# A reordered attention-and-mixer kernel: state by a casting load, dummy and half-width matmuls on TensorE, and state-token rows stored in (token, batch) order

## The chip, the cores and the metric

One core of a Trainium2 chip. The metric is device microseconds of one launch, median over runs. A launch is some 1.8 us longer than the span of its trace.

Some words of the profiles: PSUM is the memory that TensorE writes its results to, and the other engines copy (evacuate) them from there. The granted clock is TensorE's clock as a share of its full speed; in the rows of slices each digit is tenths (9 is 90% or more). The chain is the work that ended last, followed back step by step to what released it. The shape of a matmul's tile (128*128, 128*64 ...) is the part of TensorE's array that it uses.

## The reference

Eight batches, eight heads, 512 tokens and 32 state tokens of 64 features. Tokens attend to state and state attends to tokens (a softmax each); the two results are concatenated to 544 rows of 512 features, which go through a mixer:

```python
scores  = scale * x @ state.T ;  xread = softmax(scores)  @ state      # 512 rows
scores2 = scale * state @ x.T ;  sread = softmax(scores2) @ x          # 32 rows
y = concat([xread, sread], rows)                # (8, 544, 512) after merging heads
W_tok = scale * (y @ w_q) @ (y @ w_k).T         # 544 x 544 for each batch
out = relu(W_tok @ y) @ w_out                   # float32, (8, 544, 512)
```

## The kernel before

The schedule is written by hand: a list of tokens `step.batch.engine`, from which each engine gets its instructions in that order. TensorE (PE) is busy with matmuls, most of them small, for 79.8 of the 93.4 us; VectorE (DVE, `v`), ScalarE (ACT, `a`) and GpSimd (POOL, `p`) evacuate PSUM and do softmax work.

```python
ORDER = """
zst.0.p stc0.0.v stc1.0.a stt0.0.t xc0.0.p stt1.0.t xc1.0.a ste0.0.v ix1.0.p stf0.0.a xT0.0.t
stf1.0.v ix2.0.p ste1.0.a iwo.0.p xc2.0.v stb.0.t xc3.0.v ix3.0.p xTe0.0.v stbe.0.a xT1.0.t wc.0.p
...                                                             # cut
oe0.5.a fin1.6.t fin0.7.1 oe0.6.v oc0.7.a
"""
nc.sync.dma_start(out=st_f, in_=state...)         # whole state, 512 KB, (batch, head) on 64 partitions
...
def load(n, b, e):                                # ix: x of batch b, float32 to bf16 on the way
    nc.gpsimd.dma_start(out=x_bf[b], in_=xsrc(b, 0, H))
def st_tr(n, b, e):                               # 32 transposes of 64x64 for each half of the state
    ...
def st_back(n, b, e):                             # 16 transposes back, for the other layout
    ...
def fin_acc(ps, lhs):                             # one output piece: 128 rows, 512 columns
    for k in range(KC):
        nc.tensor.matmul(out=ps, lhsT=lhs(k), rhs=w_o[:, k, :], start=(k == 0), stop=(k == KC - 1))
def fs_ev(n, b, e):                               # state-token rows of four batches
    ...
    nc.sync.dma_start(out=out[4 * j : 4 * j + 4, S:SP, :], in_=ost)
```

`zst` clears a tile, `stt` and `ste/stf` transpose and evacuate the state, `xT` and `xTe` the same for x, `pt` makes scores, `exp` exponentiates, `srd` and `sums` read x by state, `wq`, `wks`, `wk`, `g`, `v`, `mix`, `mixs` are the mixer, `fin` and `fs` the output projections, `oe`, `oc`, `fse` their copies and stores.

The softmax here doesn't subtract the row's maximum and nothing guards it: scores larger than these inputs give would overflow.

## Time and profile before

| | before |
|---|---|
| time, median | 96.32 us (95.04 to 96.79); 96.0 to 96.1 us in the later sessions |
| span of the trace | 93.4 us |
| PE busy, granted clock over the span | 79.8 us (85%), 0.93 |
| batch 1's first transposes begin | 15.44 us |
| PE ends | 87.77 us |
| from there to the end | 5.6 us |

I read the last three rows as three stretches, start, middle and tail: 15.44 + 72.33 + 5.63 = 93.4.

### The profile page before, as it was taken

How to read it: one execution, taken by the hardware profiler on the slowest of the kernel's cores; microseconds unless marked ns; L12 is line 12 of the kernel's file. 1: busy time of each engine (PE TensorE's matmuls, PEld its weight loads, DVE VectorE, ACT ScalarE, POOL GpSimd, SP SyncE). 2: the span in 40 equal slices, each digit the busy share in tenths (PEclk: the TensorE clock that was granted, in tenths of full speed). 3: DMA queues.
4: the chain of work that ended last, by engine and by line, in shares of the span. 5: the costliest groups of instructions: out<-in, count | busy, mean ns of one | idle time of the engine just before them, and what ended most of it. 6: DMA issues, size and time to landing. Idle time of an engine off the chain costs nothing.

```text
span 93.4 us, 3134 instructions
## 1 busy us (share of the span) xinstructions
PE 79.8 (85%) x1376; PEld 53.4 (57%) x1376; DVE 56.2 (60%) x109; ACT 53.6 (57%) x80; POOL 44.6 (48%) x58
## 2 busy tenths in 40 slices
PE   5908098998995999999999999999999999999500
PEld 3506086896864676888366547646668644444100
DVE  1026948589584959896496198965786487222500
ACT  2324746687894687359967647864054876444200
POOL 7307994894499989899500009339750000000000
PEclk9998555599999999999999999999999999999985
DMA  1998799999999915500032517806455004428990
GB/s 28 305 260 193 94 160 156 205 203 194 197 199 197 201 18 232 225 11 0 0 130 102 225 22 213 311 30 270 186 225 232 0 0 164 173 39 300 400 363 21
DMA packets 12933, 15.13 MB, mean 162 GB/s; under 512 B 1592, under 2 KB 10296, under 8 KB 12856
## 3 DMA queue, kind: packets, MB, share of 16 engines
q0 software_dynamic: 7808, 4.19, 33.2%
q1 hardware_dynamic: 4280, 9.70, 29.3%
q10 hardware_dynamic: 832, 1.05, 3.8%
q8 instruction: 10, 0.16, 0.7%
q14 instruction: 3, 0.02, 0.1%
HBM read 10.22 MB, written 8.91 MB: 205 GB/s over the span
## 4 chain that ended last, share of the span: by engine, by line
PE 76%; ACT 6%; DMA 6%; DVE 4%; issue 2%; DVEq 0%
PE fin_ps L538 30%; PE xT_ps L246 9%; DMA st_f<-in_state_dram 6%; PE pt_ps L264 5%; PE mix_ps L504 5%; PE at_ps L322 4%; PE srd_ps L335 3%; PE wq_ps L398 3%; PE wk_ps L436 3%; DVE stT L139 3%; ACT xT L137 2%; PE fins_ps L538 2%; PE srd_ps L348 2%; PE v_ps L468 2%; PE g_ps L452 2%
## 5 line engine op out<-in xcount | busy, mean ns | idle before, releaser
L538 PE MATMUL fin_ps<-w_o,rmix 128*128 128x512 bf16 x128 | 30.0, 379 | 0.0
L309 POOL TENSOR_TENSOR A<-E,rinv 128x1024 bf16<-128x1024 bf16 (+1 forms) x9 | 15.3, 1718 | 15.5 <-DVE rinv L303 15.5
L538 PEld LDWEIGHTS <-rmix 128*128 128x128 bf16 x128 | 11.6, 98 | 12.5 <-ACT rmix L143 0.3
L137 ACT COPY ost<-fin_ps 128x1024 f32<-128x1024 f32 (+1 forms) x10 | 9.3, 928 | 14.1 <-PE fin_ps L538 13.6
L139 DVE COPY ost<-fin_ps 128x1024 f32<-128x1024 f32 (+1 forms) x8 | 8.7, 1089 | 11.1 <-PE fin_ps L538 7.5
L280 ACT ACTIVATE E<-pt_ps 128x512 bf16<-128x512 f32 x16 | 9.6, 603 | 4.3 <-PE pt_ps L264 4.3
L372 POOL TENSOR_TENSOR sbd<-srn,mask 128x256 bf16<-128x256 bf16 x16 | 9.5, 612 | 4.4 <-DVE srn L362 4.1
L295 DVE TENSOR_REDUCE rsum<-E 128x16 f32<-128x512 bf16 x16 | 10.6, 672 | 1.1 <-ACT E L280 1.1
L246 PE MATMUL xT_ps<-ident,x_bf 128*128 128x128 bf16 x128 | 11.0, 238 | 0.1
L145 DVE TENSOR_SCALAR rmix<-mix_ps 128x1024 bf16<-128x1024 f32 x7 | 8.5, 1223 | 2.7 <-PE mix_ps L504 2.6
L137 ACT COPY xT<-xT_ps 128x1024 bf16<-128x1024 bf16 x9 | 9.1, 1020 | 1.5 <-PE xT_ps L246 1.5
L143 ACT ACTIVATE rmix<-mix_ps 128x1024 bf16<-128x1024 f32 x9 | 9.3, 1032 | 0.7 <-PE mix_ps L504 0.5
L213 POOL TENSOR_TENSOR stbd<-st_bf,mask 128x256 bf16<-128x256 bf16 x16 | 9.3, 614 | 0.0
L246 PEld LDWEIGHTS <-x_bf 128*128 128x128 bf16 x128 | 8.4, 106 | 1.0 <-issue 0.4
L264 PE MATMUL pt_ps<-stT,xT 128*128 128x64 bf16 x128 | 7.1, 203 | 0.5 <-DVE xT L139 0.4
L504 PE MATMUL mix_ps<-wq,V 64*128 64x256 bf16 x64 | 5.7, 272 | 1.2 <-issue 1.1
L152 POOL DMA_DIRECT2D x_bf<-in_x_dram x7 | 6.6, 944 | 0.0
L264 PEld LDWEIGHTS <-xT 128*128 128x128 bf16 x128 | 5.6, 105 | 1.6 <-DVE xT L139 0.5
L139 DVE COPY xT<-xT_ps 128x1024 bf16<-128x1024 bf16 x7 | 4.8, 686 | 2.2 <-PE xT_ps L246 2.0
L139 DVE COPY AT<-at_ps 128x1024 bf16<-128x1024 bf16 x7 | 4.8, 685 | 1.2 <-PE at_ps L322 1.2
L322 PE MATMUL at_ps<-ident,A 128*128 128x128 bf16 x64 | 5.0, 219 | 0.0
L504 PEld LDWEIGHTS <-V 64*128 64x128 bf16 x64 | 2.4, 94 | 3.8 <-issue 2.8
(76 smaller groups left out, 115.9 us busy)
## 6 DMA issues: line engine op xcount, KB each, us to landing
out_dram<-ost SPq DMA_DIRECT2D x14, 512.0 KB, 3.8
x_bf<-in_x_dram POOLq DMA_DIRECT2D x7, 512.0 KB, 13.4
out_dram<-ost SPq DMA_DIRECT2D x4, 256.0 KB, 2.1
st_f<-in_state_dram SPq DMA_DIRECT2D x1, 512.0 KB, 5.6
x_f<-in_x_dram ACTq DMA_DIRECT2D x2, 256.0 KB, 4.3
x_f<-in_x_dram SPq DMA_DIRECT2D x2, 256.0 KB, 6.3
w_o<-in_moe_w_out_dram POOLq DMA_DIRECT2D x1, 512.0 KB, 10.5
out_dram<-ost ACTq DMA_DIRECT2D x2, 256.0 KB, 3.9
```

What stands on the lines that cost most here:

```text
L137: nc.scalar.copy(out=out, in_=in_)
L139: nc.vector.tensor_copy(out=out, in_=in_)
L143: nc.scalar.activation(out=out, in_=in_, func=AF.Relu)
L213: nc.gpsimd.tensor_tensor(out=stbd[:, b, r], in0=st_bf[:, b, r : r + 1, :].to_broadcast((128, NP, D)), in1=mask[:, :, None].to_broadcast(( ...
L246: nc.tensor.transpose(out=ps[:, u, q, :], in_=x_bf[b][:, NP * r + q, 128 * u : 128 * u + 128], identity=ident,)
L264: nc.tensor.matmul(out=ps[:, 2 * u : 2 * u + 2, NS * q : NS * q + NS], lhsT=L[b][f"xTe{r}"][:, u, q, :], rhs=stT[:, b, :, NP * r + q, :], ...
L280: nc.scalar.activation(out=L[b]["E"][:, r].rearrange("p c q n -> p c (q n)"), in_=L[b][f"pt{r}"], func=AF.Exp, scale=float(scale),)
L295: nc.vector.reduce_sum(out=L[b]["rsum"][:, w], in_=L[b]["E"].rearrange("p r c q n -> p (r c q) n")[:, w], axis=AX.X,)
L309: eng.tensor_tensor(out=L[b]["A"].rearrange("p r c q n -> p (r c q) n")[:, w], in0=L[b]["E"].rearrange("p r c q n -> p (r c q) n")[:, w], ...
L372: nc.gpsimd.tensor_tensor(out=L[b]["sbd"][:, r], in0=L[b]["srn"][:, r : r + 1, :].to_broadcast((128, NP, D)), in1=mask[:, :, None].to_broa ...
L504: nc.tensor.matmul(out=ps[:, h, kk, :], lhsT=L[b]["V"][rows, 128 * k : 128 * k + 128], rhs=L[b]["wq"][rows, 0:SH], start=True, stop=True,)
L538: nc.tensor.matmul(out=ps, lhsT=lhs(k), rhs=w_o[:, k, :], start=(k == 0), stop=(k == KC - 1))
```

## The change

The intent: shorten the start by a smaller first load of state and a shorter way of its transposes; keep PE's clock up by dummy matmuls; take fewer changes of PE's tile shape by splitting matmuls that stand beside half-width ones; spread the end; and let all DMA engines carry the state-token rows. Nearly every place in the order changes as well.

Cuts are marked by `...`; calls are shortened.

```diff
-    nc.sync.dma_start(out=st_f, in_=state...)             # 512 KB
+    st_src = state.rearrange("b (r q) n d -> (q n) (b r) d", r=2)
+    st_load(0, 1)                                         # batch 0, 64 KB; x of batch 0 follows
...
+    st_load(1, 3)                                         # 128 KB
+        elif n == "is":
+            nc.gpsimd.dma_start(out=st_bf[:, 3:B], in_=st_src[:, 6 : 2 * B])   # casting
...
-    for w in range(16):                                   # warm-up, 256 columns each
+    for w in range(8):                                    # 512 columns each
+    def fill(n, b, e):                                    # b dummy matmuls of 512 columns
+        ps = psA.tile([128, 512], FP, name="fill_ps", tag="psA")
+        for w in range(b):
+            nc.tensor.matmul(out=ps, lhsT=zero[:, 0:128], rhs=zero, start=True, stop=True)
...
+    def mm(m, out, lhsT, rhs, **kw):
+        if m == "c":                                      # two 64-column halves side by side
+            for h in range(2):
+                lh = lhsT[:, 2*h : 2*h+2, :] if len(lhsT.shape) == 3 else lhsT[:, 64*h : 64*h+64]
+                nc.tensor.matmul(out=out[64*h : 64*h+64], lhsT=lh, rhs=rhs, **kw)
...
-        nc.sync.dma_start(out=out[4*j : 4*j+4, S:SP, :], in_=ost)
+        nc.sync.dma_start(out=out[4*j : 4*j+4, S:SP, :].rearrange("b n e -> n b e"), in_=ost)
-    rmix_s = const.tile([128, 2, KC, 4, NS], BF, name="rmix_s")
+    rmix_s = const.tile([128, 2, KC, NS, 4], BF, name="rmix_s")
-    tail = ctx.enter_context(tc.tile_pool(name="tail", bufs=6))
+    tail = ctx.enter_context(tc.tile_pool(name="tail", bufs=7))
...
-zst.0.p stc0.0.v stc1.0.a stt0.0.t xc0.0.p ...            # the whole ORDER
+zst.0.p ix1.0.p stc.0.v xc1.0.a fill.1.t stt.0.c ste.0.v stbd.0.p stf.0.a xc0.0.p xc3.0.v ix2.0.p
+fill.7.t xT0.0.t xc2.0.v xTe0.0.a fill.1.t xT1.0.t is.0.p ...
+... fs.7.t mxe1.7.a fse.7.v fix1.7.t fix2.7.t oc1.7.a fix0.7.t oc2.7.a fix3.7.t oc0.7.a oc3.7.b
```

Both state-token stores now stand at the very end (`fse.3`, `fse.7`); one stood in the middle before. The last piece (`oc3.7.b`) is copied in two halves by DVE and ACT.

## The prediction

> **What bounds the kernel now.** I read the page's slices first, then the chain that ended last, then stretches of time, then the PE timeline, last the DMA view.
>
> The page's 40 slices (2.335 us each):
>
> ```profile
> PE   5908098998995999999999999999999999999500
> PEclk9998555599999999999999999999999999999985
> DMA  1998799999999915500032517806455004428990
> ```
>
> PE is busy in nearly every slice from the sixth on; it is the bound of the middle. But in slices 4 to 7 its clock is at half, and the first four and last three slices hold little useful PE work. The chain in order of time (start, length, what):
>
> ```profile
> 0.73 5.58 DMA st_f<-in_state_dram
> ...
> 7.08 0.71 PE stT_ps L180 x32
> ...
> 7.89 1.22 DVE stT L139
> 9.14 1.24 DVE stT L139
> 10.40 1.01 ACT stT L137
> 11.46 1.03 PE stb_ps L201 x16
> 12.49 0.98 PE xT_ps L246 x8
> ...
> 15.44 1.03 PE xT_ps L246 x8
> ...
> 79.94 7.81 PE fin_ps L538 x36
> 87.77 0.59 ACT ost L137
> ```
>
> So the start is a chain of latencies through the state: one 512 KB load, transposes, four evacuations, transposes back. The transposes of batch 1 begin at 15.44, where they also wait 0.3 us for their load. PE ends at 87.77, and 5.6 us of copy and store follow to 93.4. Three stretches, with busy time of PE, PEld, DVE, ACT and POOL, granted clock, DMA share and GB/s:
>
> ```profile
> 7.00:12.50 5.50, 3.02 (x89) 2.56 (x90) 4.23 (x6) 2.92 (x4) 4.85 (x7) 0.65 0.89 150
> 12.50:18.70 6.20, 5.81 (x133) 4.80 (x134) 3.62 (x8) 4.28 (x6) 4.68 (x7) 0.50 1.27 172
> 18.70:30.00 11.30, 9.72 (x290) 7.90 (x288) 8.05 (x19) 9.07 (x15) 8.69 (x13) 0.99 1.44 198
> ```
>
> From 12.5 to 18.7 PE is 94% busy at clock 0.50. From 18.7 to 30 the clock is full but PE is idle 1.6 us, with DVE, ACT and POOL at 70 to 80%. The start and the tail are what can still be won. The tail in the DMA view of 76 to 93.4 us (slices of 0.435 us), with the landing of the batch loads over the whole run:
>
> ```profile
> GB/s 0 0 0 0 0 202 386 396 221 0 33 381 188 38 19 14 24 71 99 160 207 395 396 424 443 377 414 424 405 179 424 419 386 381 254 71 5 0 0 0
> x_bf<-in_x_dram POOLq DMA_DIRECT2D x7, 512.0 KB, 13.4
> ```
>
> From about 85 to 91.5 us the stores run at some 400 GB/s: the last nine output pieces are made back to back and the queue is full when PE ends. Before that, from 81.6 to 83.8, only 14 to 160 GB/s move: that is the store of state-token rows issued at 80.58.
>
> **What the Trainium skill says.** "TensorE: Matmul & The Clock Gate", Part 1: the PE clock is 1.2 GHz by default and 2.4 GHz after about 3.4 us of sustained work. The trace agrees in the ratio: eight transposes take 0.45 us later, 1.03 us at 12.49. Part 4 of that page: transposes do not count as PE-busy in the same way. The trace fits: 12.5 to 18.7 is dense, largely transposes, and stays at 0.50. "TensorEngine Tiling (Array Packing)", Key Properties: changing tiling mode drains the array. The trace agrees, below, at about 0.10 us. "DMA: Bandwidth & Descriptors", on why a DMA increments its semaphore by 16: the slowest dimension of the access pattern limits how many of 16 engines carry it. The state-token store has 4 (batches) outermost, and its slow stretch fits four engines.
>
> **The change part by part.** PE timeline, start and duration; I take start to start as the cost:
>
> ```profile
> 36.37 0.41 PE L436 MATMUL wk_ps<-sw,AT 128*128 128x64 bf16 x8
> 36.71 0.42 PE L335 MATMUL srd_ps<-x_bf,E 128*32 128x64 bf16 x32
> 37.06 0.41 PE L398 MATMUL wq_ps<-AT,sw 128*64 128x256 bf16 x4
> 37.30 0.28 PE L407 MATMUL wq_ps<-srT,w_qk 128*64 128x32 bf16 x8
> ```
>
> The wk group takes 0.34 us before the srd group of another tile shape, 0.23 where its neighbour has its own shape: a change of shape costs 0.10. In the same way: eight 128-column transposes 0.45, pt or g 0.235, srd 0.27, four 512-column final matmuls 0.863, v 0.44, half a mix 0.22, wq with its state part 0.335.
>
> (a) State and batch 1, the start. Batch 0's state becomes a 64 KB load, batches 1 and 2 one of 128 KB, batches 3 to 7 a casting load on the GpSimd queue. The state arrives with heads and tokens on partitions, so the 64 small transposes, the four 1.0 to 1.2 us evacuations and the 16 transposes back are replaced by 32 transposes, 8 evacuations by group, and no way back. What gates the middle is batch 1. Its load was issued at 8.20 behind a GpSimd cast, and landed 7.2 us later. Now it stands directly after the memset that ends at 3.05: 5.15 us earlier. Meanwhile batch 0 must be transposed, exponentiated and summed; x of batch 0 should land by 5 to 5.5 us (1 MB without 512 KB of state in front), which leaves time. Batch 1's transposes: 15.44 - 5.15 = 10.3, say 10.4. Gain 5.0 us.
>
> (b) PE work from there. Adding the costs above over the order of the old kernel from batch 1's transposes on gives 62.3 us and 55 changes of shape at 0.10: 67.8. It took 87.77 - 15.44 = 72.3, so 4.5 us were cold clock and idle. The new order from the same point gives 65.0 us and 54 changes: 70.4. So the reordering does not save changes of shape (whole kernel: 60 before, 58 now); it adds 2.6 us there, of which 1.3 are six dummy matmuls at 0.216, 0.56 state transposes, the rest splits and work moved behind this point. A "c" step makes one 128-column matmul into two 64-column ones side by side; wks, already so, runs eight with 64 columns in 0.14, hence a pair in 0.035 against 0.029 unsplit. For 512 columns I count no difference.
>
> (c) Dummy matmuls, 23 in all, 4.96 us warm. Seventeen stand before batch 1, in waits, at no cost. I expect them to keep the clock mostly full where it was 0.50. That saves at most half of 15.44 to 18.7, 1.6 us. But earlier loads also bring earlier collisions: ACT and DVE were already at 70 to 80%, and the state's casting load (1,280 short pieces) sits between batch 2 and the output weights. I let the saved clock be eaten by such waits, plus 0.8: 4.5 + 0.8 = 5.3. PE's end: 10.4 + 70.4 + 5.3 = 86.1, against 87.77.
>
> (d) Tail. State rows in (token, batch) order have 32 outermost, so all engines carry them; both such stores now fall within the last 5 us, so this is needed as much as it is a gain. The last pieces are batch 7 alone, spread by mix and state work: about 0.25 MB per 0.9 us, 290 GB/s, under the 400. ACT's three copies with issue (0.59 + 0.36 = 0.95) exceed PE's 0.863 a piece, so ACT's half of the last piece starts some 0.3 late, is issued 0.6 after PE's end and lands 2.1 later (the median of quarter-MB stores on SP). With 1.3 for the end after landing (91.9 to 93.4 before, less the last crumbs): 4.0 against 5.6. Gain 1.6. The seventh tail buffer gains nothing: both kernels use six such tiles.
>
> Sum: 86.1 + 4.0 = 90.1 span, plus 1.8 (95.16 - 93.4 in the profiled run): 91.9, told as **92.0 us**, 4.5% under the median.
>
> **The rivals.** First, the load stream becomes the bound. Eight loads on the GpSimd queue took from 8.2 to about 33 us, 3.1 each, and DMA is full in those slices. With the state piece among them, batches 2 and 3 and the weights may be late, and PE waits to about 30 us. For it: the full DMA slices. Against it: after the first, no load was waited for. It would put PE's end at 88 to 89, the time at 94 to 95. Second, the clock stays low: one dummy of 0.2 us between steps may be too little against transposes. Running at half to 15 us costs 2 to 3 us more: 94 to 95. Third, splits cost more than counted: some 236 added matmuls by my count of the PE stream (203 more in all, 56 fewer at the start, 23 dummies). At 20 ns each that is 4.7 us, and the gain is gone: 96. The trace's 17 ns per small matmul with its weights, and the hidden weight loads of long ones, speak against it. On the good side, if the clock holds and the early waits vanish, 89.
>
> **Range and chances.** The old kernel's own runs spread over 1.8%. Rival one or two alone ends near the 2% line (94.4); both together, or the third, pass it. I take 89.3 to 94.8; faster 0.82, within 2% 0.15, slower 0.03.
>
> **What would show it.** Batch 1's transposes at 10 to 11 us; clock near full from 6 us on; final matmuls of batch 0 at 26 to 28 (31.05 before); PE's end near 86; 4 us behind it with no long 400 GB/s stretch. Wrong if PE waits on a load for over 3 us, if the clock is 0.5 after 12 us, or if split groups take longer than their pairs.

## More of the kernel before

What PE waited for most in the trace before (engine, line, releaser: us in total, times, longest):

```profile
PE stT_ps L180 <- DVE st_in L139: 2.4, 1, 2.4
PE stb_ps L201 <- ACT stT L137: 2.4, 1, 2.4
PE mix_ps L504 <- issue: 1.1, 1, 1.1
```

The two long waits belong to the state: for its cast, and for its evacuation before it is transposed back. There is no long wait on a load of x in the list of PE's waits.

## The result, and the profile after

Ratios here are the mean time of one kernel's fast runs over that of the other's of the same rounds, so not quite the ratio of the medians that are quoted. The changed kernel took 88.69 us (88.47 to 89.09, 4 runs) against 96.56: ratio 0.927, 95% interval 0.919 to 0.936. Run again unedited in a later session it took 89.56 (88.32 to 90.33), ratio 0.924. The direction came out as forecast, and with it the outcome that I held most likely. The first median lies 0.6 us under the low end of my range (89.3); the repeat lies just inside.

| | before | after | predicted |
|---|---|---|---|
| batch 1's transposes begin | 15.44 | 11.65 | 10.4 |
| from there to PE's end | 72.33 | 71.27 | 75.7 |
| PE's end to the end | 5.63 | 4.08 | 4.0 |
| span | 93.4 | 87.0 | 90.1 |

So between these two traces, of 6.4 us, 3.8 came from the start, 1.1 from the middle, 1.5 from the tail. The page's slices of the changed kernel (2.175 us each):

```profile
PE   4999999999999999999999999999999999999910
PEclk9999999999999999999999999999999999999996
DMA  0899999999609999995600464201461663566782
```

The dip of the clock to 5 in slices 4 to 7 is gone, and PE is busy from the second slice to the last two. Pieces of the chain that ended last, in order of time (start, us, what):

```profile
4.79 0.43 PE fill_ps L155
5.21 0.35 PE stT_ps L215 x3
5.57 2.29 PE fill_ps L155 x7
7.86 0.45 PE xT_ps L174 x8
...
11.81 0.45 PE xT_ps L174 x8
...
79.42 3.47 PE fin_ps L163 x16
82.92 0.44 DVE ost L144
83.38 0.37 ACT ost L142
```

PE is on the chain nearly throughout: where loads, casts and evacuations of state stood before, dummy matmuls (`fill_ps`) stand now. In this execution PE came to full speed late: the eight warm-up matmuls of 512 columns took 3.59 us, 0.45 each, and the seven dummies 2.29, 0.33 each, where later ones take 0.22. In the profile of another kernel below with the same start (nosplit) the seven took 1.62 and batch 1 began at 10.57. Of nine profiles with dummies this one has the slowest seven. The view of the clock shows 1.00 all the same, so before about 7 us I go by the durations. The last 9-piece run of final matmuls has become a run of four pieces. The last two lines lie one behind the other, DVE's half and then ACT's half of the last piece, although the change means them to lie side by side. (ACT was in any case still issuing the store before until 83.33.) Stretches (busy PE, PEld, which is PE's loading of weights, DVE, ACT, POOL, each with its count of instructions, then clock, DMA share, GB/s):

```profile
5.00:11.65 6.65, 6.60 (x68) 3.71 (x69) 4.13 (x10) 2.91 (x5) 5.59 (x8) 1.00 1.36 218
11.65:18.70 7.05, 6.58 (x156) 5.05 (x157) 5.46 (x14) 4.99 (x9) 6.43 (x10) 1.00 1.52 195
18.70:30.00 11.30, 11.19 (x302) 8.75 (x304) 8.80 (x20) 10.22 (x16) 11.26 (x14) 1.00 0.81 103
```

Between 18.7 and 30 us PE idles 0.1 us where it idled 1.6, though ACT is busier (10.2 of 11.3) and POOL has no pause. The tail, in the DMA view of 78.5 to 87 us (slices of 0.21 us):

```profile
GB/s 58 405 424 366 424 424 366 0 260 414 357 203 0 67 376 386 415 357 395 366 299 366 405 270 0 328 376 395 318 352 323 337 39 0 0 0 0 0 0 0
```

While data moves the rate is again near 400 GB/s, but there are gaps down to 0 until 83.8: the queue drains between stores, and only the last pieces are left over when PE ends. Before, the rate had no such gaps from 85 us on.

### The profile page after: what moved, and what is told of

It is laid out like the page before. It is cut to its first block, busy times and chain, and to the rows that moved or that the text cites. A ratio compares the mean times of both kernels' runs of the same rounds, so it can differ in the third digit from the quotient of the medians.

```text
span 87.0 us, 3553 instructions
## 1 busy us (share of the span) xinstructions
PE 80.8 (93%) x1572; PEld 53.4 (61%) x1579; DVE 52.4 (60%) x111; ACT 55.9 (64%) x83; POOL 45.1 (52%) x58
## 3 DMA queue, kind: packets, MB, share of 16 engines
q10 hardware_dynamic: 1120, 1.44, 4.6%
## 4 chain that ended last, share of the span: by engine, by line
PE 90%; ACT 4%; issue 1%; DVE 1%
PE fin_ps L161 20%; PE fin_ps L163 12%; PE fill_ps L155 6%; PE xT_ps L174 5%; PE mix_ps L541 5%; PE warm_ps L132 4%; PE srd_ps L369 3%; PE xT_ps L170 3%; PE at_ps L174 3%; PE v_ps L505 3%; PE pt_ps L163 2%; PE g_ps L163 2%; PE fins_ps L163 2%; PE wq_ps L433 2%; PE v_ps L514 2%; PE wk_ps L163 2%
## 5 line engine op out<-in xcount | busy, mean ns | idle before, releaser
L346 POOL TENSOR_TENSOR A<-E,rinv 128x1024 bf16<-128x1024 bf16 (+1 forms) x9 | 15.4, 1717 | 12.8 <-DVE rinv L340 12.5
L161 PE MATMUL fin_ps<-w_o,rmix 128*64 128x512 bf16 x160 | 19.4, 380 | 0.0
L142 ACT COPY ost<-fin_ps 128x1024 f32<-128x1024 f32 (+2 forms) x13 | 11.2, 864 | 11.6 <-PE fin_ps L161 5.9
L161 PEld LDWEIGHTS <-rmix 128*64 128x64 bf16 x160 | 8.4, 110 | 6.2 <-issue 0.6
L163 PE MATMUL fin_ps<-w_o,rmix 128*128 128x512 bf16 x44 | 11.0, 379 | 0.2
L155 PE MATMUL fill_ps<-zero 128*128 128x512 bf16 x21 | 7.8, 432 | 0.1
L150 DVE TENSOR_SCALAR rmix<-mix_ps 128x1024 bf16<-128x1024 f32 x4 | 4.9, 1222 | 3.4 <-PE mix_ps L541 3.4
L163 PEld LDWEIGHTS <-rmix 128*128 128x128 bf16 x48 | 4.3, 98 | 4.0 <-ACT rmix L148 0.2
L174 PE MATMUL xT_ps<-ident,x_bf 128*128 128x128 bf16 x80 | 6.0, 219 | 0.2 <-ACT E L317 0.2
L174 PEld LDWEIGHTS <-x_bf 128*128 128x128 bf16 x80 | 5.1, 98 | 1.3 <-issue 0.5
L132 PE MATMUL warm_ps<-zero 128*128 128x512 bf16 x8 | 3.6, 631 | 1.2 <-DVE mask L133 1.2
```

What stands on the lines that cost most here:

```text
L142: nc.scalar.copy(out=out, in_=in_)
L155: nc.tensor.matmul(out=ps, lhsT=zero[:, 0:128], rhs=zero, start=True, stop=True)
L161: nc.tensor.matmul(out=out[64 * h : 64 * h + 64], lhsT=lh, rhs=rhs, **kw)
L163: nc.tensor.matmul(out=out, lhsT=lhsT, rhs=rhs, **kw)
L174: nc.tensor.transpose(out=out, in_=in_, identity=ident)
L346: eng.tensor_tensor(out=L[b]["A"].rearrange("p r c q n -> p (r c q) n")[:, w], in0=L[b]["E"].rearrange("p r c q n -> p (r c q) n")[:, w], ...
```

## The experiments

Twelve kernels, in three sessions of four, each session on another chip; within one session they share the runs of the kernel before. Times in us, then the ratio to the kernel before with its interval. For runs of one core, "slow" means over 1.5% above the fastest run of the same kernel. The ratios leave slow runs out: two of four of the unedited changed kernel (ctrl), two of four without dummies, four of six of the earliest load, three of six of both tries together. Where a wait comes and goes from run to run, they so measure the executions without it.

### The changed kernel as it is

> The changed kernel unedited, as the measure for the runs beside it on the same chip. All theories: 88.5 to 89.1 us, span near 87.0, clock 0.99, no wait of PE longer than 0.5 us between 5 us and its end near 82.9.

89.56, ratio 0.924 [0.917, 0.931]. The profiled run was a slow one of 90.03 us, with this wait, which the first trace of the same kernel does not have:

```profile
PE xT_ps L174 <- DMA x_bf<-in_x_dram: 1.9, 1, 1.9
```

My expectation of no wait over 0.5 us was wrong. When batch 1's casting load lands varies from execution to execution of one program, and there is no margin for it: here PE was ready at 10.6 us and had to wait.

### State-token rows in the old order

```diff
-        nc.sync.dma_start(out=out[4*j : 4*j+4, S:SP, :].rearrange("b n e -> n b e"), in_=ost)
+        nc.sync.dma_start(out=out[4*j : 4*j+4, S:SP, :], in_=ost)      # and rmix_s as before
```

> The changed kernel with the state-token rows written in (batch, token) order again, four batches outermost. Theory (the two stores then run on few of the DMA engines, and now lie in the last 5 us): each takes 4 us or more to land instead of 2.4, the second lands after 84.5 and holds up the last stores on its engines; time up by 1 to 2 us, 89.7 to 90.7. Rival (they land beside the last stores anyway, hidden): within 0.4 us.

94.43, ratio 0.982 [0.977, 0.987]: slower than the changed kernel of the same session by 4.9 us in the medians, by 5.8 in the means of fast runs. The direction is the theory's; the size is more than twice the most that it allowed. PE ends at 82.5 (82.9 in the changed kernel), but 10.9 us follow instead of 4.1. The DMA view of 78.5 to 93.4 us (slices of 0.37 us), and from the view of the whole run the issues with count, KB each, and us from issue to landing:

```profile
GB/s 396 429 297 33 33 11 11 22 55 66 110 181 203 335 341 327 330 338 294 187 151 160 272 74 77 63 60 72 74 50 33 49 52 49 49 44 14 0 0 0
```

```profile
out_dram<-ost ACTq DMA_DIRECT2D x3, 256.0 KB, 8.6
...
out_dram<-ost SPq DMA_DIRECT2D x1, 128.0 KB, 9.1
out_dram<-ost ACTq DMA_DIRECT2D x1, 128.0 KB, 8.6
```

For the last 5 us before the data ends some 30 to 80 GB/s move. In the changed kernel the same ACT stores land in 2.1 us and the last halves in 2.2. I read it so: a store is done only when its slowest engine is, and each of the five stores behind the two narrow ones has a share on the crowded engines too, so all of them land late. The expectation had counted the narrow stores alone. Part of the loss is in the issue: the last ACT store took 2.24 us to be issued, against 0.34 in the changed kernel. While the narrow stores are alone, the DMA share (the last number but one, mean over the core's 16 engines) fits four of them, as long as an engine's packets don't overlap, which they do elsewhere (shares over 1):

```profile
79.60:80.40 0.80, 0.80 (x6) 0.35 (x4) 0.12 (x1) 0.51 (x1) 0.00 (x0) 1.00 0.26 31
80.40:81.00 0.60, 0.60 (x5) 0.25 (x4) 0.00 (x0) 0.16 (x2) 0.00 (x0) 1.00 0.25 10
```

But 10 to 31 GB/s is far less than a quarter of the 400 that all of them reach, so the number of engines is not the whole reason. What else slows them stays open.

### The new row order in the kernel before

The same two lines the other way round, in the kernel before, nothing else.

> The kernel before with only the state-token rows in (token, batch) order. Theory (its second such store, issued at 80.58, holds a few DMA engines till about 86, and the stores behind it wait for just these engines): the last store lands at about 90.5 instead of 92, 1.0 to 1.6 us faster. Rival (my prediction's reading: the tail is limited by the 400 GB/s of all engines together): within 0.4 us, since no byte less is moved.

94.82 against 95.98, ratio 0.992 [0.986, 0.997]. Faster, by 0.8 us; the interval, 0.3 to 1.3 us, excludes no gain at all, but reaches both the theory's 1.0 and the rival's "within 0.4". The profiles speak for the theory: PE ends at 87.70 (87.77 before), and the tail is 4.9 us instead of 5.6. So by these two traces about half of what the whole change gains in the tail is had by this one line. In the new order the same line is worth 5 to 6 us; there two such stores stand among the last seven.

### Without the dummy matmuls

ORDER without its `fill` tokens; the eight warm-up matmuls stay.

> The changed kernel without its 23 dummy matmuls in gaps (the eight warm-up matmuls at the start stay). Theory A (the dummies hold the clock): the clock falls to 0.5 for several us between 7 and 18 us, as it did in the kernel before, and the time rises by 2 to 3 us to 90.7 to 92. Rival B (the loads and the chain of latencies set the start, the dummies only fill waits, and the clock is held by the other work): no change within 0.5 us. Rival C (PE is the bound from 5 us on, so that the dummies lie on its path): the time falls by 1.3 to 2.5 us to 86.2 to 87.5 at full clock.

89.98, ratio 0.927 [0.921, 0.933], against 0.924 [0.917, 0.931] of the unedited kernel beside it: no difference that these runs can tell (0.3%, with intervals of 0.6 to 0.7% to either side). Rival C, that the dummies cost 1.3 us or more, falls, and so does the size of theory A. The half of A about the clock holds. A stretch of the profile (a fast run):

```profile
12.50:15.00 2.50, 2.50 (x40) 2.50 (x33) 0.97 (x4) 2.25 (x4) 2.50 (x4) 0.50 1.74 194
```

The clock falls to 0.50 there, where it is 1.00 with dummies. But batch 1's transposes begin at 10.69, not held up by dummies (PE waits 0.5 us for the load; with dummies and an early full speed it was 10.57), and from there to PE's end it is 72.2 us against 71.3. In these two executions the later start and the fuller clock cancel: span 87.0 both times.

### Dummies alone, in the kernel before

28 of them: 9 while it waits for the state, 10 before the transposes back, one before each of nine groups.

> The kernel before with 28 dummy matmuls of 512 columns: 9 while it waits for the state, 10 before the transposes back, and one ahead of each of nine groups up to batch 1's scores. Theory (the clock is held full): 12.4 to 18.7 no longer at 0.5; batch 1's transposes still wait for their load at 15.4, so 0.5 to 1.5 us faster. Rival (the dummies cost what they save, or the clock falls all the same): within 0.4 us.

96.99, ratio 1.006 [0.996, 1.016]: the rival's "no gain". The slices of its clock (a slow run):

```profile
PEclk9999999999996699999999999999999999999997
```

The dip in slices 4 to 7 is filled (a smaller one comes later, at some 29 to 33 us), and yet batch 1's transposes begin at 15.78 (15.44 before) and PE ends at 89.65. Up to the transposes back (11.79, against 11.46 before) the clock was not what bounded the kernel before; the waits for state, casts and evacuations were. From there to batch 1's transposes the full clock did shorten the work, but five dummies of 0.22 us and a wait of 0.6 us for a PSUM buffer took the place of what it saved; a second such wait follows. So the runs show that dummies do not pay there, not that the clock is worth nothing; the details are of this one slow execution.

### Batch 1's load early, alone in the kernel before

```diff
-zst.0.p stc0.0.v ... xc0.0.p ... ste0.0.v ix1.0.p
+zst.0.p ix1.0.p stc0.0.v ... xc0.0.p ... ste0.0.v
```

> The kernel before with only batch 1's casting load issued first, directly behind the memset on GpSimd, at about 3 us instead of 8.2. Rival (my prediction's step a: this load gates the middle, and its issue 5 us earlier brings 5 us): 3 to 5 us faster. Theory (in the kernel before the state chain and the half clock gate just as much, PE waited 0.3 us for that load): 0 to 0.7 us faster.

95.48, ratio 0.999 [0.992, 1.005]. Step (a) of my prediction, that this load "gates the middle" of the kernel before, is not borne out: issued 5 us earlier, it leaves batch 1's transposes at 14.97 (a fast run):

```profile
14.97 1.03 PE L246 MATMUL xT_ps<-ident,x_bf 128*128 128x128 bf16 x8
```

### Batch 1's load late, in the changed kernel

```diff
-zst.0.p ix1.0.p stbd.0.p xc0.0.p ix2.0.p       # GpSimd's own order
+zst.0.p stbd.0.p xc0.0.p ix1.0.p ix2.0.p
```

> The changed kernel with only batch 1's load put back behind the GpSimd cast of batch 0, at about 5 us instead of 3. Theory (with the state chain short, this load is what PE would wait for): its landing and with it batch 1's transposes come 1.2 to 2.5 us later, and the time rises by 1 to 2.5 us over the changed kernel's 88.3 to 90. Rival (PE's own dummies and the first batch gate): within 0.4 us.

90.56, ratio 0.942 [0.934, 0.950], against 0.924 and 0.927 for the changed kernel in the other sessions: 1.6 to 2.0% slower, or 1.4 to 1.8 us, as the theory has it (across sessions, and with intervals that touch in one of the two). In the profile (a slow run) PE waits for the load, and the transposes begin at 12.98:

```profile
PE xT_ps L174 <- DMA x_bf<-in_x_dram: 1.8, 1, 1.8
```

Together with the run before: the early load is worth nothing that these runs can tell alone and some 1.6 us once the state's chain is short. That the ctrl profile has a like wait at the normal place shows that part of this wait also comes by chance. The comparison of fast runs leaves out just those runs of ctrl; with all runs counted the means are 90.3 us here against 88.7 and 89.4, so 0.9 to 1.6 us. The direction stands, the size is uncertain.

### The whole state in one load first

512 KB in one plain load at the head, cast by DVE, no casting load of state; the rest as in the changed kernel.

> The changed kernel with the whole state in one plain 512 KB load at the head of the queue, as before, and cast by VectorE; no casting load of state. Theory (batch 0's start waits for the first bytes of state, so a small first load matters): batch 0's transposes of state come about 2.5 us later, its x too; batch 1's load gates at about 11 to 12.5, so part is hidden: 0.5 to 2 us slower than the changed kernel's 88.5 to 89.6. Rival (only the early batch 1 load and the shorter way of the state count): within 0.4 us, or faster by up to 1 us since 1,280 short pieces less go over the GpSimd queue.

91.36, ratio 0.947 [0.941, 0.954]: 2.1 to 2.6% slower, or 1.9 to 2.3 us, at or just over the upper end of the theory's range. Batch 0's state is cast at 5.95 instead of 3.67. The profile is of a slow run and shows other delays too (a wait of 1.6 us for a load further on, a lower clock in two slices), so how much of the loss is the later first state, and how much the moved cast and the queue behind it, stays open.

### No splits

Every step marked `c` made whole again, except the state's transposes, which are half-width by nature.

> The changed kernel with every matmul and transpose that it splits into two 64-column halves made whole again; the order stays. By my count this order then changes the shape of PE's tiles 77 times instead of 58. Theory (splits pay by avoiding changes of shape): 19 x 0.10 us = 1.9 us more, less some 0.6 us for pairs of small matmuls that become single ones: time up by 1.0 to 1.9 us, 89.7 to 90.6. Rival (splits cost instruction and weight-load time, as my prediction feared, and the changes of shape are hidden in other work): time down by 0.5 to 2 us, 86.7 to 88.2.

89.70, ratio 0.932 [0.927, 0.938] against 0.924 [0.917, 0.931]: 0.9% slower by the means, with intervals that just overlap. The profile (fast) tells more. From batch 1's transposes to PE's end, without splits (first line) and with them:

```profile
10.57:83.40 72.83, 71.60 (x1255) 46.50 (x1266) 46.74 (x92) 51.00 (x75) 35.33 (x42) 1.00 0.71 166
11.65:82.92 71.27, 70.35 (x1497) 48.52 (x1501) 46.86 (x94) 50.49 (x75) 35.25 (x41) 1.00 0.70 167
```

PE is busy 1.25 us longer without splits, at full clock in both, as the theory says (1.0 to 1.9). The whole stretch is 1.5 us longer, but this execution also began it 1.1 us earlier and then has 2.5 us of ACT's work on its chain, so not all of that is due to the splits. Without splits this order changes PE's tile shape 77 times instead of 58. The costs that I feared of splits are small: in the chains sixteen half-width score matmuls take 0.25 us and eight whole ones 0.23, sixteen half-width row sums 0.29 and eight whole ones 0.18.

### Two tries to do better

First, batch 1's load ahead even of GpSimd's memset.

> The changed kernel with batch 1's load ahead of GpSimd's 1.8 us memset, so issued at about 1.2 instead of 3.0. Theory (its landing gates and scatters the start): batch 1's transposes never wait for it, runs scatter less, 0.3 to 1.3 us faster. Rival (it takes bandwidth from batch 0's x and state, which then gate): same or up to 1 us slower.

92.45 (89.8 to 95.7), ratio 0.939 [0.932, 0.945]: slower and far more scattered (only two of six runs count as fast), the rival's direction and about or beyond its size. In the profile (slow) the plain load of 128 KB of state landed 8.2 us after issue, against 5.0 in the changed kernel, and PE waited for its cast:

```profile
PE stT_ps L215 <- DVE st_bf L144: 2.0, 1, 2.0
```

Second, the last piece in two PSUM buffers so that ACT's half need not wait for DVE's, and the piece before it copied by DVE and stored by SP:

> The changed kernel with the last output piece in two PSUM buffers of 256 columns, so that ACT's half no longer waits for VectorE's (in the changed kernel it does: 83.38 begins as 82.92 ends), and the piece before it copied by VectorE and stored by SP. Theory: the last store is issued some 0.45 us earlier, 0.3 to 0.6 us faster. Rival (the end is set by bytes in flight): within 0.2 us.

88.91 (87.9 to 91.47), ratio 0.920 [0.915, 0.926]. From PE's end to the end of the span it is 3.9 us in the profile (a slow run), against 4.1 in the unedited kernel; DVE is now busy with the piece before when its half is ready. That is the rival's 0.2 us, and no gain that the times can prove. Both together:

> Both of the two edits before in one kernel. If they are independent and both theories hold: 0.6 to 1.8 us faster than the changed kernel. If the early load hurts, it is slower than the tail edit alone by as much as the early load alone is slower.

90.89 (89.55 to 93.68), ratio 0.937 [0.931, 0.944]: as slow as the early load alone. Its profile is of a fast run and shows the same delay: the 128 KB load landed after 7.5 us, and PE waited 0.9 us for its cast. No kernel here is shown to be faster than the changed one.

## Why the prediction was right or wrong

**Direction and size.** Faster by over 2% was right. The forecast gain was 4.5%, the measured one 7.3 to 7.6%.

**Step (a), the start: right in outcome, wrong in cause.** I gave 5.0 us and it was 3.8. I named one gate, batch 1's load. In the kernel before that load was not a gate by itself (b_ix1, no gain), nor did filling up the clock help (b_fill, no gain). The state's chain gated as well, and after the change both were shortened. Put back one at a time, the late load costs some 1.6 us (0.9 to 1.6 with all runs counted) and the old first load of state, with what moved beside it, some 2 us. My 10.3 us for the first use of batch 1 came true in one profile (nosplit, which is the same program up to there: 10.57). It left out that the load's landing varies, and that PE's own speed at the start does: where it came up late, the dummies before batch 1, meant to stand "in waits, at no cost", held PE. So the changed kernel began batch 1's transposes at 11.65 in one execution (PE slow until about 7 us), at 12.55 in another (the load late).

**Steps (b) and (c), the middle: the term that failed.** "I let the saved clock be eaten by such waits, plus 0.8: 4.5 + 0.8 = 5.3." The work itself, 70.4 us, was sized well: PE was busy for 70.35 of the 71.27 us that the stretch took, at a clock of 1.00, so clock and idle together were 0.9 us, not 5.3. This term alone is 4.4 us; with the 1.25 us of the later start against it, it is the 3.2 us by which PE ended early (82.9 against 86.1). I had feared collisions from ACT and DVE at 70 to 80%. They ran at up to 90% and PE idled less; batch 0's first final matmul came at 24.6 us, before the 26 to 28 that I gave. That the new order places work that is ready is my reading of it, which no run tests; I had taken no credit for the order beyond counted work. "No difference" for long split matmuls was right, and the 58 changes of shape were counted right, but I compared them with the 60 of the old order and so overlooked what the splits are for: this order without them has 77.

**Step (d), the tail: right in sum, by luck in part.** 4.0 us were predicted, 4.1 measured, but two errors of 0.3 us cancel: the last store was issued 0.9 us after PE's end and not 0.6, and 1.0 us and not 1.3 followed its landing. The seventh buffer has no part in it: six tiles are used. "Needed as much as it is a gain" was right, but I gave the row order no size. In the new order it is worth 5 to 6 us, in the old 0.8. My sum of the ACT copies had the last half start 0.3 us late for the copies' sake; it started 0.46 late, when ACT's issue of the store before (83.33) and DVE's half were both just done.

**The rivals.** The load stream (first rival) does appear, as waits of 1.8 to 1.9 us in slow executions, but not as the bound. The low clock (second) does not: 1.00 from 7 us to PE's end, and only the first 7 us slow in the durations. Costly splits (third) do not.

**Readings that were off.** I called 12.5 to 18.7 us of the kernel before "largely transposes": they are 3.0 of 5.8 busy us, and two idle waits of 2.4 us come before, so the low clock there may as well come from these; no run separates the two. The ratio of the clock should have been taken from start to start, 0.83 us for eight transposes then and 0.45 later; 1.03 is the duration of a view. And the 14 to 160 GB/s run to 84.7 us, not 83.8.

**What stays open.** The share of the order itself cannot be separated: no run has the old order with the new state, or the reverse. Nor is it settled what the dummies are worth, beyond that the runs with and without them differ by 0.3%, less than their scatter. Nor is it known why the narrow stores move so little.

## What to carry to other kernels

When several chains meet at the start, lift one in an experiment before you call it the gate: here the early load, the clock and the state's chain each looked like one, and the two that were lifted alone (the clock by dummies that cost time themselves) gave nothing. For a store, look at the outermost dimension of its access pattern before you look at its bytes: here two stores of 256 KB with four rows outermost went with late landings of every store behind them. And when you sum the work of a reordered PE stream, size the idle term from what makes each engine's next step ready, not by carrying the old idle time over.

## What the Trainium skill lacked or had wrong

- "DMA: Bandwidth & Descriptors" says which dimension limits the number of engines, and to keep it a multiple of 16. It does not say what a narrow store does to those behind it: five full-width stores landed after 6.4 to 9.7 us instead of 2.0 to 2.4, with some 30 to 80 GB/s moving at the end, 5 to 6 us of the kernel. The traces show rates and shares, not which engines.
- "TensorEngine Tiling (Array Packing)", Key Properties, says that a change of tiling mode drains the array, without a figure. Read from start to start it is about 0.10 us here, and 19 changes less went with 1.25 us less busy time of PE.
- "TensorE: Matmul & The Clock Gate" says that transposes do not count as busy in the same way, but not how much other work keeps the clock. With dummies of 512 columns (0.22 us each) between groups of 0.2 to 0.5 us up to 14 us it was 1.00 from 7 to 18.7 us; without them it was 0.50 from 12.5 to 15 us.
- No page that I read gives a figure for how much a large casting load delays plain loads issued about the same time: issued at 1.44 instead of 2.99 us, it went with a 128 KB load landing after 7.5 (fast run) and 8.2 us (slow run) instead of 4.4 to 5.0.
